# Chunked attention feeding a gated feed-forward layer: attn @ v joined with the next tile's scores, the last output tile in halves, and a new order of the plan

## The chip, the cores and the metric

The kernel runs on one core of a Trainium2 chip. The metric is the device time of one execution in microseconds (us), the median of three runs. TensorE (PE) does the matmuls, and PEld its weight loads; VectorE (DVE), ScalarE (ACT) and GpSimd (POOL) work element by element; SyncE (SP) only issues DMA transfers.

## The reference

```python
# q, k, v: (8, 8, 576, 64); chunks of 64 positions attend only to themselves
scores = scale * np.matmul(q_c, k_c.transpose(0, 1, 2, 4, 3))
scores = scores - np.max(scores, axis=-1, keepdims=True)
attn = np.exp(scores)
attn = attn / (np.sum(attn, axis=-1, keepdims=True) + 1e-09)
out = np.matmul(attn, v_c)
...
# x = out with the heads side by side: (8, 576, 512)
h = np.maximum(x @ w_in, 0.0)                 # (8, 576, 1024)
for k in range(K):                            # K = 3, a depthwise convolution along the sequence
    conv_out += conv_w[k][None, None, :] * hp[:, k:k + S, :]
gate = 1.0 / (1.0 + np.exp(-conv_out))
return (h * gate @ w_out).astype(np.float32)
```

## The kernel before

The 4608 rows of the sequence are cut in two ways. The attention and the output go in 36 **tiles** of 128 rows (two chunks of 64). The first product of the feed-forward layer, with its convolution and gate, goes in 16 **units** of 288 rows (half a batch), each in eight blocks f of 128 hidden channels.

A tile of attention is a chain of steps over all engines. Its q and k are loaded and transposed (`t_pe` on PE and `t_copy` on ACT for tiles 0 to 8, `t_dve` on DVE for the rest). Then come `scores` (16 matmuls of 64x64 on PE, line 171), `s_max` and `s_sub` on DVE, `s_exp` on ACT, `s_sum`, `s_eps` and `s_rec` on DVE, `s_norm` on POOL (line 203), `p_pe` (a transpose on PE, line 210), `p_copy` on ACT, `attn_v` (16 more matmuls of 64x64, line 223), and `x_hi` on ACT and `x_lo` on DVE (line 251), which write the result as a rounded part and a rest into `x_h` and `x_l`. The scores and the result of attn @ v live in the two halves of one PSUM tile, `sx`.

Block (u, f) is `mm1` (12 matmuls of 290 columns, line 260: three products of the split parts, four pieces of the contraction each). It then goes through ACT, DVE, ACT, DVE (`h_relu`, `c_mid`, `c_left`, `c_right`, `c_sig`, `c_mul`), and `g_hi` (ACT) and `g_lo` (POOL) split it into `g_h` and `g_l`. `mm1` of unit u waits for `x_lo` of every tile that the unit reads (tiles 0 to 2 for unit 0, 0 to 4 for unit 1). It holds one of six PSUM banks until `c_mul` is done. Output tile t takes eight steps `mm2` (three matmuls of 512 columns each, line 313), one for each f; when all are done, ACT copies the bank (`o_copy`, line 318) and SP stores it (`o_store`).

The weights come in over SP (`w_load`) and are split into high and low parts by six steps on DVE (lines 342 to 368), ACT and POOL. w_in comes in six pieces, in the order of the plan, and the last of them that SP issues is called wi3 here; w_out comes in four.

The order of all this is not left to the program text. Every step is entered with an engine, an estimated cost and a key. A planner then walks through the steps and gives each engine, at each time, the ready step with the lowest key; `by_step` and `by_chain` are tables of numbers that shift the keys by kind of step and by tile, block or output tile. `kinds` and `turn` charge PE for passing between 64x64 matmuls, transposes and large matmuls, and the key of a 64x64 step is lowered by 6 when the last step on PE was one too. Each engine then executes its instructions in the planned order, strictly. Where PE is idle in the plan and a bank is free, the program puts in transposes of the identity that nobody reads (line 685, called fillers here), until the first `mm2`:

```python
    pe_free, until_ = 2.0, min(begin[i] for i in range(n_) if steps[i]["fn"] is mm2)
    ...
            for _ in range(int((begin[i] - pe_free) / 0.14) if idle else 0):
                nc.tensor.transpose(out=banks[idle[-1]][:, 0:P], in_=ident, identity=ident)
```

Of the kernel before, what the change touches and what calls it, by code (L numbers as in the profile page):

```python
# [30 lines left out]
def attn_ffn(ctx: ExitStack, tc: tile.TileContext, q, k, v, w_in, conv_w, w_out, out):  # L31
    nc = tc.nc
    B, H, S, D = q.shape
    DM, DF = w_in.shape
# [194 lines left out]

    def x_views(st, t, x):  # L230
# [193 lines left out]
    def att(t, key, load_key, writes):  # L424
# [19 lines left out]
        s = step("PE", 0.47, key, scores, (st,), tt + [before.get("s")], take=[("sx", st, "s")], free=["qT", "kT"], bank="sx")  # L444
# [73 lines left out]

    for u in range(NU + 1):

        for t in tiles_for[u] if u < NU else []:
# [27 lines left out]
        "w_load": -4.5, "w_mask": -6, "w_bias": -5.5, "w_rest": -5, "w_low": -2, "w_sign": -9.5, "w_pow": -6,  # L549
        "<lambda>": -7, "c_sum": -23.5, "c_pe": 5, "c_copy": -31.5, "w_hi": 12, "w_lo_big": 20, "load_rows": -11,  # L550
        "t_pe": -7.5, "t_copy": -11, "load_v": 10.5, "scores": -3, "s_max": 8, "s_sub": -21.5, "s_exp": -9, "s_sum":
        -0.5, "s_eps": 2.5, "s_rec": 10, "s_norm": -19, "p_copy": -0.5, "attn_v": 4, "x_hi": -3, "x_lo": -6, "mm1":
        -0.5, "h_relu": -4.5, "c_mid": 2, "c_left": 2.5, "c_right": 2.5, "c_sig": 5, "c_mul": 6, "g_hi": 3, "g_lo":
        29.5, "o_copy": 6, "o_store": 16.5, "load_group": 35.5, "load_part": -3.5, "t_dve": 23
# [165 lines left out]
```

## Time and profile before

| | |
|---|---|
| median of 3 runs | 516.85 us (516.49 to 519.48) |
| profiled execution | 517.22 us, of which the span of the instructions is 515.4 us |
| busy share of the span | PE 98%, PEld 87%, DVE 68%, ACT 63%, POOL 33% |
| matmuls | 5104, at a mean granted clock of 0.999 |

The span runs from the first to the last instruction; the remaining 1.8 us of the execution lie around it. A share of busy time is a mean over stages that differ: in the first 90 us weights are split and DVE is nearly always busy, and afterwards PE is.

### The profile page before, as it was taken

What the parts mean: (1) busy time and instruction counts of PE and PEld (TensorE: products, weight loads), DVE (VectorE), ACT (ScalarE), POOL (GpSimd) and SP (SyncE); (2) the same over time, 40 slices, a digit from 0 to 9 for tenths busy, and PEclk for the clock granted to TensorE, in tenths of its full rate; (3) what the DMA queues carried; (4) which work ended last, traced back from release to release, by engine and by line L of the source; (5) the groups of instructions that cost most, each with busy time, mean ns of one, the idle gap of its engine ahead of it and who ended that gap; (6) DMA issues with size and microseconds to landing.
All of it is one profiled execution on the core that took longest, in us unless ns stands there. A gap on an engine that the chain in (4) does not pass through costs nothing.

```text
span 515.4 us, 13095 instructions
## 1 busy us (share of the span) xinstructions
PE 505.4 (98%) x5104; PEld 450.8 (87%) x5104; DVE 351.8 (68%) x732; ACT 325.1 (63%) x783; POOL 172.1 (33%) x237
## 2 busy tenths in 40 slices
PE   8898999999999999999999999999999999999997
PEld 8788988888998899899888898889889898988985
DVE  5779999668749588867854499727858585753320
ACT  4678998845866367757635487737746567755430
POOL 1424485532314323532511153314313315043220
PEclk9999999999999999999999999999999999999999
DMA  8889751543325545523455554343551211001101
GB/s 218 198 218 262 187 131 37 93 100 88 51 46 117 89 114 108 98 47 51 100 114 113 123 89 85 57 97 74 97 121 33 61 23 42 2 1 43 41 14 68
DMA packets 183170, 47.04 MB, mean 91 GB/s; under 512 B 175404, under 2 KB 175428, under 8 KB 183108
## 3 DMA queue, kind: packets, MB, share of 16 engines
q1 hardware_dynamic: 183108, 46.20, 40.5%
q8 instruction: 40, 0.66, 0.6%
q14 instruction: 22, 0.18, 0.1%
HBM read 36.72 MB, written 9.44 MB: 90 GB/s over the span
## 4 chain that ended last, share of the span: by engine, by line
PE 85%; DVE 8%; DMA 3%; ACT 2%; POOL 1%; issue 0%; SPq 0%; DVEq 0%; ACTq 0%; POOLq 0%
PE b_ps L313 38%; PE b_ps L260 37%; PE sx_ps L223 4%; PE sx_ps L171 3%; DMA qk<-in_moe_w_in 3%; PE b_ps L210 3%; DVE wt L360 1%; DVE wv L355 1%; POOL wv L376 1%; DVE wv L351 1%; DVE we L368 1%; DVE c L281 1%; DVE wt L342 1%; DVE c L290 1%; DVE x_l L251 1%; DVE c L275 1%
## 5 line engine op out<-in xcount | busy, mean ns | idle before, releaser
L304 POOL TENSOR_TENSOR g_l<-c,g_h 128x288 fp32r<-128x288 f32 (+8 forms) x184 | 114.7, 638 | 217.3 <-ACT g_h L300 209.8
L313 PE MATMUL b_ps<-wo_h,g_h 128*128 128x512 f32 x288 | 118.1, 410 | 0.0
L313 PE MATMUL b_ps<-wo_h,g_l 128*128 128x512 f32 x288 | 113.3, 393 | 0.0
L313 PE MATMUL b_ps<-wo_l,g_h 128*128 128x512 f32 x288 | 112.9, 392 | 0.0
L275 DVE SCALAR_TENSOR_TENSOR c<-b_ps,cw,c 128x288 f32<-128x288 f32 (+1 forms) x128 | 65.2, 512 | 62.7 <-ACT c L271 62.4
L260 PE MATMUL b_ps<-x_h,wi_h 128*128 128x290 f32 x512 | 91.5, 300 | 1.3 <-DVE c L290 1.3
L260 PE MATMUL b_ps<-x_l,wi_h 128*128 128x290 f32 x512 | 90.2, 298 | 0.0
L260 PE MATMUL b_ps<-x_h,wi_l 128*128 128x290 f32 x512 | 89.8, 297 | 0.0
L260 PEld LDWEIGHTS b_ps<-x_h,wi_h 128*128 128x128 f32 x512 | 77.3, 189 | 6.2 <-DVE c L290 2.3
L266 ACT ACTIVATE b_ps<-b_ps 128x290 f32<-128x290 f32 x128 | 50.7, 398 | 47.1 <-PE b_ps L260 46.4
L300 ACT CAST g_h<-c 128x288 fp32r<-128x288 f32 (+8 forms) x184 | 60.3, 358 | 26.9 <-DVE c L290 13.3
L260 PEld LDWEIGHTS b_ps<-x_h,wi_l 128*128 128x128 f32 x512 | 76.4, 190 | 0.0
L260 PEld LDWEIGHTS b_ps<-x_l,wi_h 128*128 128x128 f32 x512 | 76.3, 189 | 0.0
L290 DVE SCALAR_TENSOR_TENSOR c<-c,b_ps 128x288 f32<-128x288 f32 x128 | 57.2, 449 | 20.5 <-ACT c L287 18.8
L287 ACT ACTIVATE c<-c 128x288 f32<-128x288 f32 x128 | 56.5, 443 | 22.7 <-DVE c L281 21.5
L281 DVE SCALAR_TENSOR_TENSOR c<-b_ps,cw,c 128x287 f32<-128x287 f32 (+1 forms) x128 | 65.4, 514 | 2.9
L271 ACT ACTIVATE c<-b_ps,cw 128x288 f32<-128x288 f32 x128 | 63.3, 498 | 4.7 <-POOL g_l L304 0.4
L313 PEld LDWEIGHTS b_ps<-wo_h,g_l 128*128 128x128 f32 x288 | 54.1, 188 | 12.2
L203 POOL TENSOR_TENSOR e<-e,z 128x512 f32<-128x512 f32 x36 | 38.1, 1062 | 75.8 <-DVE z L200 62.5
L313 PEld LDWEIGHTS b_ps<-wo_h,g_h 128*128 128x128 f32 x288 | 54.2, 188 | 10.3
L313 PEld LDWEIGHTS b_ps<-wo_l,g_h 128*128 128x128 f32 x288 | 54.2, 188 | 8.6
L181 DVE TENSOR_REDUCE m<-sx_ps 128x8 f32<-128x512 f32 x36 | 24.6, 683 | 22.3 <-PE sx_ps L171 21.4
(48 smaller groups left out, 513.1 us busy)
## 6 DMA issues: line engine op xcount, KB each, us to landing
v<-in_v SPq DMA_DIRECT2D x144, 64.0 KB, 2.6
out<-wt SPq DMA_DIRECT2D x36, 256.0 KB, 2.4
qk<-in_q SPq DMA_DIRECT2D x96, 48.0 KB, 2.3
qk<-in_k SPq DMA_DIRECT2D x96, 48.0 KB, 2.3
qk<-in_moe_w_out SPq DMA_DIRECT2D x4, 1024.0 KB, 7.7
qk<-in_q SPq DMA_DIRECT2D x96, 24.0 KB, 1.9
qk<-in_k SPq DMA_DIRECT2D x96, 24.0 KB, 1.9
qk<-in_moe_w_in SPq DMA_DIRECT2D x4, 512.0 KB, 5.1
```

The lines of the kernel that those rows point to most:

```text
L181: nc.vector.tensor_reduce(out=st["m"], in_=st["sv"], op=ALU.max, axis=AX.X)
L203: nc.gpsimd.tensor_tensor(out=st["e"], in0=st["e"], in1=st["z"].rearrange("p (h o) -> p h o", o=1).broadcast_to([P, H, C]), op=ALU.mult)
L260: nc.tensor.matmul(h_ps[:, 0:XU], lhsT=wt[:, f // 2, kt, P * (f % 2):P * (f % 2) + P], rhs=xt[:, u % NX, kt, :], start=n == 0, stop=n == 3 ...
L266: nc.scalar.activation(out=banks[st["h"]][:, 0:XU], in_=banks[st["h"]][:, 0:XU], func=AF.Relu)
L271: nc.scalar.mul(out=st["c"], in_=banks[st["h"]][:, i0:i0 + HS], mul=cw[:, FT + f:FT + f + 1])
L275: nc.vector.scalar_tensor_tensor(out=c[:, a:HS], in0=banks[st["h"]][:, i0 + a - 1:i0 + HS - 1], scalar=cw[:, f:f + 1], in1=c[:, a:HS], op0 ...
L281: nc.vector.scalar_tensor_tensor(out=c[:, 0:b], in0=banks[st["h"]][:, i0 + 1:i0 + 1 + b], scalar=cw[:, 2 * FT + f:2 * FT + f + 1], in1=c[: ...
L287: nc.scalar.activation(out=st["c"], in_=st["c"], func=AF.Tanh, scale=0.5)
L290: nc.vector.scalar_tensor_tensor(out=st["c"], in0=st["c"], scalar=1.0, in1=banks[st["h"]][:, st["i0"]:st["i0"] + HS], op0=ALU.add, op1=ALU ...
L300: nc.scalar.copy(out=g_h[:, f, gs], in_=st["c"][:, cs])
L304: nc.gpsimd.tensor_tensor(out=g_l[:, f, gs], in0=st["c"][:, cs], in1=g_h[:, f, gs].bitcast(F32), op=ALU.subtract)
L313: nc.tensor.matmul(banks[st["o"]], lhsT=gt[:, f, o:o + P], rhs=wt[:, f, :], start=f == 0 and n == 0, stop=f == FT - 1 and n == 2)
```

## The change

From tile 8 on (`BOTH = 7`: the pair begins with attn @ v of tile 6 and the scores of tile 7), `scores` of a tile is no longer a step of its own. A step `both` issues the 16 matmuls of `attn_v` of the tile before and right behind them the 16 of `scores`; it is ready only when both are, and takes both halves of `sx`. Output tile 35 is computed in two halves of 256 columns, each in a bank of its own with its own copy and store. Fillers may go in until 110 us of the plan instead of until the first `mm2`. The planner takes two buffers of one pool for one step. All tables of keys are new, and steps whose key lies before 110 have a table of their own, which was a copy of the other before.

```diff
+    BOTH = 7
...
+    def both(st, before_):
+        attn_v(before_)
+        scores(st)
...
-    def mm2(st, t, f):
+    def mm2(st, t, f, m0=0, m1=DM):
         o = P * t % GR
         for n, (gt, wt) in enumerate(((g_h, wo_h), (g_h, wo_l), (g_l, wo_h))):
-            nc.tensor.matmul(banks[st["o"]], lhsT=gt[:, f, o:o + P], rhs=wt[:, f, :],
+            nc.tensor.matmul(banks[st["o"]][:, 0:m1 - m0], lhsT=gt[:, f, o:o + P], rhs=wt[:, f, m0:m1],
...
-        s = step("PE", 0.47, key, scores, (st,), tt + [before.get("s")], take=[("sx", st, "s")], free=["qT", "kT"], bank="sx")
+        after, take = tt + [before.get("s")], [("sx", st, "s")]
+        if t < BOTH:
+            s = step("PE", 0.47, key, scores, (st,), after, take=take, free=["qT", "kT"], bank="sx")
+        else:
+            b, tb, after_b, writes_b = before["x"]
+            s = step("PE", 0.94, key, both, (st, b), after + after_b, take=[("sx", b, "x")] + take,
+                     free=["qT", "kT", "pT", "v"], bank="sx")
+            x_steps(b, tb, s, key, writes_b)
...
+            cols = [(0, DM)] if t < NT - 1 else [(0, DM // 2), (DM // 2, DM)]
...
     by_step = {
-        "w_load": -4.5, "w_mask": -6, "w_bias": -5.5, "w_rest": -5, "w_low": -2, "w_sign": -9.5, "w_pow": -6,
+        "w_load": 23, "w_mask": -4, "w_bias": 24.5, "w_rest": 13, "w_low": -40.5, "w_sign": -28, "w_pow": -38,
...
     by_chain = [
-        9, -224, -167, -36, 12, -10, -96, 17, 35, 24, 31, 60, -46, -46, -16, 24, 26, 58, 8, -2, 35, 14, 36, 41, 0, -2,
+        -145, 322, -84, -153, -153, -69, -66, -56, -34, -30, -6, -21, -100, -74, -68, -10, -29, -22, -43, -62, -17, -54,
...
-    pe_free, until_ = 2.0, min(begin[i] for i in range(n_) if steps[i]["fn"] is mm2)
+    pe_free, until_ = 2.0, 110.0
```

What this does to the order, in three places. First, PE, around the scores of tile 9. Before, the scores of a tile (64x64 with kT and qT) can stand alone between large matmuls:

```order
L210 MATMUL b_ps<-ident,e 128x128 x4
L313 MATMUL b_ps<-wo_h,g_h 128x512
L313 MATMUL b_ps<-wo_l,g_h 128x512
L313 MATMUL b_ps<-wo_h,g_l 128x512
L171 MATMUL sx_ps<-kT,qT 64x64 x16
L313 MATMUL b_ps<-wo_h,g_h 128x512
```

After, they always follow attn @ v (64x64 with pT and v):

```order
L318 MATMUL b_ps<-wo_h,g_h 128x512
L318 MATMUL b_ps<-wo_l,g_h 128x512
L318 MATMUL b_ps<-wo_h,g_l 128x512
L224 MATMUL sx_ps<-pT,v 64x64 x16
L172 MATMUL sx_ps<-kT,qT 64x64 x16
L318 MATMUL b_ps<-wo_h,g_h 128x512
```

The 72 steps of this kind (36 of each) form 48 runs on PE before, of which 24 are pairs, and 42 after, of which 30 are.

Second, SP, the loads up to the last piece of w_in, wi3 (the last row of each). Before, it is issued behind the rows of tile 4 (loads of 64 partitions), another half piece of w_in and v of tile 2:

```order
L330 DMA qk<-in_moe_conv_w 24x256
L109 DMA qk<-in_q 64x8x64 x2
L109 DMA qk<-in_k 64x8x64 x2
L330 DMA qk<-in_moe_w_in 128x2x512
L141 DMA v<-in_v 64x4x64 x4
L330 DMA qk<-in_moe_w_in 128x4x512
```

After, the same loads stand ahead of it in another order; the other whole piece of w_in has come close to it, v of tile 2 and the rows of tile 4 lie between:

```order
L335 DMA qk<-in_moe_w_in 128x2x512
L110 DMA qk<-in_q 128x8x64
L110 DMA qk<-in_k 128x8x64
L335 DMA qk<-in_moe_w_in 128x4x512
L142 DMA v<-in_v 64x4x64 x4
L110 DMA qk<-in_q 64x8x64 x2
L110 DMA qk<-in_k 64x8x64 x2
L335 DMA qk<-in_moe_w_in 128x4x512
```

Third, ACT at the end of the program. Before, after the last blocks' steps, four output tiles are copied:

```order
L287 ACTIVATE c<-c 128x288
L300 CAST g_h<-c 128x160
L300 CAST g_h<-c 128x128
L318 ACTIVATE wt<-b_ps 128x512 x4
L716 UNCONDITIONAL_BRANCH
```

After, the two halves of tile 35 stand ahead of two whole tiles, 33 and 34, which end the program:

```order
L292 ACTIVATE c<-c 128x288
L305 CAST g_h<-c 128x160
L305 CAST g_h<-c 128x128
L323 ACTIVATE wt<-b_ps 128x256 x2
L323 ACTIVATE wt<-b_ps 128x512 x2
L740 UNCONDITIONAL_BRANCH
```

## Rows read from the trace of the kernel before

**Rows 1.** The page's chain of work that ended last: shares of the span by engine.
```profile
PE 85%; DVE 8%; DMA 3%; ACT 2%; POOL 1%; issue 0%; SPq 0%; DVEq 0%; ACTq 0%; POOLq 0%
```
**Rows 2.** Windows: busy us by engine (instructions), then clock, DMA share, GB/s.
```profile
0.00:37.07 37.07, 33.33 (x476) 30.56 (x477) 27.19 (x56) 22.81 (x40) 11.77 (x15) 1.00 0.88 212
37.07:59.57 22.50, 20.72 (x243) 19.75 (x242) 20.31 (x38) 19.05 (x42) 8.88 (x8) 1.00 0.84 216
59.57:90.00 30.43, 29.82 (x295) 26.06 (x294) 30.06 (x60) 26.68 (x57) 20.52 (x16) 1.00 0.46 112
90.00:511.44 421.44, 421.41 (x4099) 374.46 (x4097) 274.25 (x582) 255.96 (x647) 130.90 (x200) 1.00 0.35 72
```
**Rows 3.** What PE waited for, whole span: us in total, times, longest.
```profile
PE b_ps L260 <- DVE c L290: 1.3, 2, 0.8
PE b_ps L210 <- POOL e L203: 1.1, 2, 1.0
```
**Rows 4.** Timeline of PE: first blocks of unit 0, and the first of unit 1.
```profile
37.07 0.78 PE L260 MATMUL b_ps<-x_h,wi_h 128*128 128x290 f32 x4
37.69 0.71 PE L260 MATMUL b_ps<-x_l,wi_h 128*128 128x290 f32 x4
38.23 0.70 PE L260 MATMUL b_ps<-x_h,wi_l 128*128 128x290 f32 x4
...
59.57 0.65 PE L260 MATMUL b_ps<-x_h,wi_h 128*128 128x290 f32 x3
```
**Rows 5.** Timeline of DVE before the two starts of Rows 4.
```profile
36.33 0.84 DVE L251 TENSOR_TENSOR x_l<-sx_ps,x_h 128x136 fp32r<-128x136 f32 x3 [0.40 <-ACT x_h L247]
38.85 0.69 DVE L342 TENSOR_SCALAR wt<-qk 128x1024 uint32<-128x1024 uint32 x1 [1.69 <-DMA qk<-in_moe_w_in]
...
59.17 0.75 DVE L251 TENSOR_TENSOR x_l<-sx_ps,x_h 128x256 fp32r<-128x256 f32 x2
```
**Rows 6.** Timeline of PE: a lone `p_pe` and a lone `scores` between steps of `mm2`.
```profile
115.97 0.60 PE L210 MATMUL b_ps<-ident,e 128*128 128x128 f32 x4
116.32 0.48 PE L313 MATMUL b_ps<-wo_h,g_h 128*128 128x512 f32 x1
116.63 0.40 PE L313 MATMUL b_ps<-wo_l,g_h 128*128 128x512 f32 x1
116.87 0.39 PE L313 MATMUL b_ps<-wo_h,g_l 128*128 128x512 f32 x1
117.19 0.69 PE L171 MATMUL sx_ps<-kT,qT 64*64 64x64 f32 x32
117.82 0.50 PE L313 MATMUL b_ps<-wo_h,g_h 128*128 128x512 f32 x1
118.15 0.39 PE L313 MATMUL b_ps<-wo_l,g_h 128*128 128x512 f32 x1
```
**Rows 7.** Timeline of PE: two 64x64 steps side by side.
```profile
145.03 1.16 PE L223 MATMUL sx_ps<-pT,v 64*64 64x64 f32 x64
146.12 0.50 PE L313 MATMUL b_ps<-wo_h,g_h 128*128 128x512 f32 x1
146.46 0.39 PE L313 MATMUL b_ps<-wo_l,g_h 128*128 128x512 f32 x1
```
**Rows 8.** One window of Rows 2's view, where DMA was idle in part.
```profile
22.00:28.00 6.00, 5.72 (x102) 4.94 (x101) 5.72 (x14) 4.76 (x9) 3.25 (x3) 1.00 0.54 110
```
**Rows 9.** Timeline of PE and POOL: tile 12 from its scores to `p_pe`.
```profile
160.74 0.69 PE L171 MATMUL sx_ps<-kT,qT 64*64 64x64 f32 x32
161.36 0.50 PE L313 MATMUL b_ps<-wo_h,g_h 128*128 128x512 f32 x1
...
165.21 1.04 POOL L203 TENSOR_TENSOR e<-e,z 128x512 f32<-128x512 f32 x1
...
166.31 0.66 PE L210 MATMUL b_ps<-ident,e 128*128 128x128 f32 x4
```
**Rows 10.** Timeline of ACT: the last copy of an output tile.
```profile
511.70 0.60 ACT L318 ACTIVATE wt<-b_ps 128x512 f32<-128x512 f32 x1 [0.78 <-PE b_ps L313]
```

More of the change, by code (lines that the diff above doesn't have):

```diff
@@ L543, in attn_ffn @@
-            s = step("ACT", 0.58, key + 1, o_copy, (st,), [prev], take=["wt"], free=[("bk", "o")])
-            step("SP", 1.2, key + 2, o_store, (st, t), [s], free=["wt"], lag=0.8)
-    by_step_early = {
-        "w_load": -4.5, "w_mask": -6, "w_bias": -5.5, "w_rest": -5, "w_low": -2, "w_sign": -9.5, "w_pow": -6,
[L550 to L554, printed above, removed]
+            units = [v_ for v_ in range(NU) if HS * v_ < P * t + P and P * t < HS * v_ + HS]
@@ new lines, in attn_ffn @@
+            cols = [(0, DM)] if t < NT - 1 else [(0, DM // 2), (DM // 2, DM)]
+            for n, (m0, m1) in enumerate(cols):
+                st = {}
+                prev = None
+                for f in range(FT):
+                    key = U[u + 1] + (U[u + 2] - U[u + 1]) * (i + (n + f / FT) / len(cols)) / len(outs_in[u]) + 0.3
+                    prev = step("PE", 0.7 / len(cols), key, mm2, (st, t, f, m0, m1),
+                                [prev] + wo_done[f] + [g_done[v_, f] for v_ in units], take=[("bk", st, "o")] if f == 0 else [])
+                    mm2_of[t, f] = prev
+                s = step("ACT", 0.58 if n == 0 == len(cols) - 1 else 0.38, key + 1, o_copy, (st, m1 - m0), [prev], take=["wt"], free=[("bk", "o")])
+                step("SP", 1.2, key + 2, o_store, (st, t, m0, m1), [s], free=["wt"], lag=0.8 / len(cols))
@@ new lines, in attn_ffn @@
+    by_step_early = {
+        "w_load": -7.5, "w_bias": -3, "w_rest": 2, "w_low": 2.5, "w_sign": 1.5, "w_pow": -12, "<lambda>": 9.5, "c_sum":
+        10, "c_pe": 23, "c_copy": -4.5, "w_hi": 15.5, "w_lo_big": 1, "w_lo_copy": 12.5, "load_rows": -3.5, "t_pe": -7,
+        "t_copy": -6.5, "load_v": 1.5, "scores": 4.5, "s_max": 7, "s_sub": 8.5, "s_exp": -8, "s_sum": -6, "s_eps": -0.5,
+        "s_norm": 15.5, "p_pe": -1, "p_copy": -4, "attn_v": 11.5, "x_hi": 9, "x_lo": 4.5, "mm1": -5, "h_relu": 1.5,
+        "c_mid": 3.5, "c_left": 3.5, "c_right": 5, "c_sig": -1, "c_mul": 8, "g_hi": 0.5, "g_lo": -3.5, "mm2": 5,
+        "o_copy": -40, "o_store": -1.5, "both": 14, "load_group": 20, "load_part": -11, "t_dve": -25.5
@@ L562, in attn_ffn @@
-        29.5, "o_copy": 6, "o_store": 16.5, "load_group": 35.5, "load_part": -3.5, "t_dve": 23
+        "w_load": 23, "w_mask": -4, "w_bias": 24.5, "w_rest": 13, "w_low": -40.5, "w_sign": -28, "w_pow": -38,
+        "<lambda>": 11.5, "c_sum": -7.5, "c_pe": 7.5, "c_copy": 20, "w_hi": 19, "w_lo_big": -19, "w_lo_copy": -7.5,
+        "load_rows": 15, "t_pe": -0.5, "t_copy": 27, "load_v": -11.5, "scores": -11.5, "s_max": 9, "s_sub": 11, "s_exp":
+        1.5, "s_sum": 2.5, "s_eps": -5.5, "s_rec": -6.5, "s_norm": -32.5, "p_pe": -2, "p_copy": -3, "attn_v": -25,
@@ L563, in attn_ffn @@
+        "x_hi": -21.5, "x_lo": -1.5, "mm1": -1, "h_relu": -13.5, "c_mid": -1.5, "c_left": -3, "c_right": 2, "c_sig":
+        6.5, "c_mul": 2, "g_hi": -5, "g_lo": -26, "mm2": 1, "o_copy": -17, "o_store": 5, "both": -0.5, "load_group":
+        -14, "load_part": 31.5, "t_dve": 27.5
     }
     by_chain = [
[10 rows of a table removed]
[10 rows of a table added]
     ]
```

51 lines of the change are left out of this document (23 added, 28 removed), and 18 rows, old and new, of the table by_chain.

## The prediction

> **What bounds the kernel now.** I read the chain of waits first: 85% of the span lies on PE [rows 1]. The windows by stage then show which stage this holds for. From 90 us to the end of the matmuls PE is busy for 421.41 of 421.44 us, and the list of what PE waited for has only start-up entries [rows 2, 3]. From there nothing but PE's own work counts: how many matmuls there are, and what each change of shape costs. Before 90 us it is otherwise: from 59.57 to 90 DVE is busy for 30.06 of 30.43 us, and between 37.07 and 59.57 PE waits or runs fillers [rows 2, 3]. The two starts that matter there are set by DVE: the first block of unit 0 starts at 37.07, when `x_lo` of tile 2 (36.33, three instructions) ends, and unit 1 at 59.57, beside `x_lo` of tile 4 (59.17) [rows 4, 5]. DVE itself stood idle for 1.69 us before 38.85, until wi3, the last piece of w_in, had landed [rows 5]. So three things can move the time: the start of unit 1, PE's work from there on, and the tail.
>
> **PE's work: the 64x64 steps.** A lone `scores` begins 0.32 after the start of the matmul ahead of it, where 0.23 is the usual spacing (0.09 more), lasts 0.63 until the next start, and the next matmul takes 0.33 instead of 0.23: 0.09 + 0.63 + 0.10 = 0.82 [rows 6]. Two steps side by side take 1.09, and the next matmul 0.34; with the same 0.09 ahead that is 1.29 [rows 7]. A merge saves 2 x 0.82 - 1.29 = 0.35. The change makes 29 joined steps, but most tiles had a neighbour already: counted from the first block of unit 1, the order has 61 such steps in 39 runs before and in 32 after. Seven merges at 0.35 are **-2.45**. On the same stretch stand 33 transposes (`p_pe`, `t_pe`) before and 35 after; a lone one costs 0.35 + 0.08 = 0.43 [rows 6], so **+0.9**. Ten of them lean on a 64x64 step before and three after; each then shares a change of shape, about half of 0.09, so **+0.3**. Together **-1.2**. All of it is on the path, since PE never waits there. Changes between `mm1` and `mm2` have become more frequent, but both are 128x128 and I price them at 0: between the bounds of 0 and 0.1 for a few tens of them, since in [rows 6] only the other shapes lengthen a neighbour.
>
> **The halved tile.** 24 matmuls of 512 columns become 48 of 256. Four matmuls of 290 columns start 0.54 apart (38.23 - 37.69), 0.135 each [rows 4], and one of 512 takes 0.23 [rows 6]: 0.095 for 222 columns, 0.43 ns each, which leaves 0.01 us for the matmul itself. One of 256 is then 0.121, and 48 x 0.121 - 24 x 0.23 = **+0.3**. The ends: 0, if only columns count, and 48 x 0.135 - 5.5 = +1.0, if it is no faster than one of 290. I take 0.3, as both rows lie near. The Trainium skill (TensorEngine Tiling (Array Packing), section Instruction Overhead) gives about 60 cycles for each matmul; 24 more at 2.4 GHz would make an estimated 0.6 instead of 0.3, which these rows do not show. At the end the halves bring nothing: the order puts both of their copies ahead of the whole tiles 33 and 34. The last copy is again one of 512 columns, at 511.70 for 0.60 [rows 10], with a whole store behind it, so the tail keeps its length. The extra `o_copy` and `o_store` run on ACT and SP, which are idle in part there [rows 10]; if they were late, only banks would come free later, with no block left that needs one.
>
> **The start of unit 1.** It hangs on `x_lo` of tile 4, and that on DVE's queue from wi3's first step on. In both orders DVE has exactly the same instructions ahead of that step. Between it and `x_lo` of tile 4 there are 36 before, from 38.85 to 59.92, so 21.1 us or 0.58 each [rows 5], and 40 after: three long ones of w_out have gone, seven (two blocks' convolution and product, one `w_pow`) have come. This is between 0 and 4 x 0.58 = 2.3; six of the seven being short, I take **+0.7**. When wi3 lands is open. SP issues the same loads ahead of it in both orders. From 22 to 28 us DMA had a busy share of 0.54 [rows 8], so 6 x 0.46 = 2.8 us went unused; with the hole closed wi3 lands up to 2.8 earlier, with no change 0, and if the rows of tile 4, now directly ahead of it, hold SP up, about 1 later. I take half of the hole, **-1.4**. The start of unit 1 then moves by **-0.7**, between -2.8 and +1.7. PE reaches unit 0 sooner, by the fewer fillers in the order (158 ahead of it instead of 167, and one `scores` less), but waits the longer for unit 1: nothing of that comes through. Fillers themselves cost nothing as long as PE would wait. The later limit for them is empty: the order has none after unit 1 begins, before or after.
>
> **New waits.** `both` makes `scores` wait for `p_copy` of the tile before. Behind it on PE stand large matmuls that could have run; behind those, everything. The chain from the end of tile 12's scores (161.36) to its `p_pe` (166.31) takes 4.95, of which `s_norm` is the last 1.04 [rows 9], and PE had just enough other work between. In the new order, counted at the prices above, the shortest such distances are 4.4 (tiles 17 and 19), 4.8, 5.1, 5.1 and 5.3: waits of 0.55, 0.55 and 0.15 if the chain is as long. The bounds are 0 and 1.2; I take **+0.6**, since that chain had other work of DVE in it. Between 59.57 and 90 PE lost 30.43 - 29.82 = 0.6 [rows 2]; I leave it, with 0 and 2 as ends, since two pieces of w_out are now split later on DVE and the `mm2` that need them stand later too.
>
> **Sum.** -1.2 + 0.3 - 0.7 + 0.6 = -1.0 on the profiled execution of 517.22, so 516.2; that execution lay 0.37 above the median of 516.85, so 515.8 for the median. With all ends on one side it would be -4.6 or +4.7.
>
> **Rivals.** (1) *The start comes through whole.* wi3 lands 2.8 earlier, DVE follows without a hole, the 0.6 of waits before 90 us goes and no new wait comes: -1.2 + 0.3 - 2.8 - 0.6 = -4.3, or 512.5, and a little more if DVE's stretch is shorter than I think. For it speaks that the loads are in another order and that the hole is there; against it, that the loads of tile 4, with 64 partitions, lie in the hole and are still ahead of wi3. (2) *The chain of a joined step becomes the bound, slower.* `p_pe` waits for `s_norm`, behind it on PE stand the blocks, and the next `both` waits too. It decides from a chain longer than 4.95. With 6.0, the seven distances below that (4.4 to 5.8) cost 7.2 in all; with that in place of the 0.6 the sum is +5.6, or 522.4. For it speaks that DVE has other instructions between these steps; against it, that DVE is busy for only 274 of 421 us after 90 [rows 2], and that tile 12 had interruptions too. (3) *PE's clock falls in the start.* With 11 fewer fillers PE may stand idle for longer, and a lower clock would double the 8 blocks of unit 0: 8 x 1.62 = 13, less the 3 to 4 us of waits and fillers there, +9, or 526. The granted clock was 1.00 in each stage, also where PE waited for 1.0 at a time [rows 2, 3], which speaks against it. The Trainium skill (TensorE: Matmul & The Clock Gate, section Why this matters for your kernels) warns that an idle TensorE returns to half rate; by that rule only this rival would come about. (4) *The change does not do what it says*: the halves are not last, and the fillers' limit is without effect. Both are in the forecast already.
>
> **How the numbers follow.** The forecast has a chance of 0.72 and, with the bounds of its terms taken together in part, reaches from 513 to 519.5; rival 1 has 0.19, rival 2 0.07, rival 3 0.02. The range has to reach down to rival 1: 512.2 to 519.5. One per cent, 5.2 us, is about what a measurement of this kernel can tell from no change; below 511.7 lies about half of rival 1, 0.10, and above 522.0 most of rivals 2 and 3 and a little of the forecast's upper tail, 0.06. The rest is 0.84.
>
> **What would show it.** Right: unit 1 begins at 57 to 60 us, 32 runs of 64x64 steps after that, each pair at 1.29 with its neighbours; 48 matmuls about 0.12 apart for tile 35; a tail of 4 us after the last matmul, as before. PE's list of waits after 90 us holds about 0.6 us, under `s_norm`. Wrong: unit 1 before 56 us or after 62, long waits of `p_pe` for POOL, matmuls of 256 columns at over 0.14, or a granted clock below 1.00 before 90 us.

## The result, and the profile after

| | before | changed |
|---|---|---|
| median, us (20 executions each) | 517.0 (516.23 to 519.48) | 518.24 (516.21 to 520.42) |
| ratio to before, 95% interval | | 1.0022 [1.0012, 1.0033] |
| the same, measured again beside the experiments, twice | | 1.0034 [1.0018, 1.0050] and 1.0020 [1.0004, 1.0035] |
| profiled execution: time, span | 517.22, 515.4 | 519.21, 517.3 |
| first block of unit 0, of unit 1 | 37.07, 59.57 | 37.80, 61.63 |

The changed kernel is a little slower: 0.2 to 0.3%, inside the 1% that I called no difference and inside the range, but on the other side of the forecast. The page's chain of work that ended last has less PE and more DVE than in [rows 1]:

```profile
PE 83%; DVE 11%; DMA 2%; ACT 1%; issue 1%; POOL 1%; POOLq 0%; DVEq 0%; ACTq 0%
```

The windows by stage, cut at the same events as [rows 2], columns as there:

```profile
0.00:37.80 37.80, 32.91 (x436) 29.94 (x436) 26.27 (x54) 21.02 (x37) 10.10 (x15) 0.95 0.88 211
37.80:61.63 23.83, 20.61 (x265) 19.23 (x264) 22.68 (x44) 21.08 (x46) 13.18 (x9) 1.00 0.72 176
61.63:90.00 28.37, 27.71 (x289) 24.77 (x288) 28.23 (x53) 25.98 (x54) 18.73 (x15) 1.00 0.53 137
90.00:513.31 423.31, 422.94 (x4136) 377.76 (x4134) 277.19 (x585) 258.23 (x648) 132.88 (x201) 1.00 0.34 72
```

The second stage took 23.83 instead of 22.50, and DVE was busy in it for 22.68 instead of 20.31: DVE, not PE, set its end. In the first the granted clock was 0.95, where it had been 1.00. From unit 1 to the end of the last matmul it is 451.7 against 451.9 before: there the change is worth nearly what the forecast's other terms said together.

What PE waited for in the whole span (total, times, longest):

```profile
PE b_ps L211 <- POOL e L204: 3.5, 3, 2.6
PE b_ps L211 <- DVE c L295: 1.3, 1, 1.3
PE b_ps L265 <- DVE c L295: 1.1, 1, 1.1
```

Against [rows 3] a long wait for `s_norm` is new, 2.65 us. It stands in the start, ahead of `p_pe` of tile 0. The timeline of PE from there:

```profile
20.37 0.65 PE L211 MATMUL b_ps<-ident,e 128*128 128x128 f32 x4 [2.65 <-POOL e L204]
...
22.20 1.06 PE L150 MATMUL b_ps<-ident,qk 128*128 128x128 f32 x4
23.18 1.13 PE L224 MATMUL sx_ps<-pT,v 64*64 64x64 f32 x32
24.25 2.22 PE L709 MATMUL b_ps<-ident 128*128 128x128 f32 x12
26.40 0.69 PE L172 MATMUL sx_ps<-kT,qT 64*64 64x64 f32 x32
```

And two windows of the same stretch (the granted clock is the third number from the right):

```profile
22.00:24.00 2.00, 1.98 (x35) 1.61 (x37) 1.66 (x4) 1.25 (x3) 1.27 (x1) 0.57 0.97 253
24.00:26.00 2.00, 2.00 (x22) 1.88 (x19) 0.99 (x3) 1.61 (x3) 0.05 (x1) 0.57 1.18 237
```

After the wait the granted clock is 0.57, most of the time at the lower of its two levels (1.2 GHz): four transposes take 1.06 instead of 0.60, `attn_v` 1.13 instead of 0.69. This was rival 3's mechanism, and the first suspect.

The timeline of DVE ahead of wi3's first step and at `x_lo` of tile 4, for [rows 5]:

```profile
37.27 0.83 DVE L256 TENSOR_TENSOR x_l<-sx_ps,x_h 128x136 fp32r<-128x136 f32 x3
38.02 0.68 DVE L186 TENSOR_TENSOR e<-sx_ps,m 128x512 f32<-128x512 f32 x1
39.39 0.69 DVE L195 TENSOR_REDUCE z<-e 128x8 f32<-128x512 f32 x1 [0.70 <-ACT e L191]
40.00 0.68 DVE L347 TENSOR_SCALAR wt<-qk 128x1024 uint32<-128x1024 uint32 x1
...
61.25 0.74 DVE L256 TENSOR_TENSOR x_l<-sx_ps,x_h 128x256 fp32r<-128x256 f32 x2
```

The timeline of PE at the first block of unit 1, for [rows 4]:

```profile
61.63 0.79 PE L265 MATMUL b_ps<-x_h,wi_h 128*128 128x290 f32 x4
```

The wait of 1.69 for wi3 is gone. But `w_mask` of wi3 comes at 40.00, not earlier than 38.85; and from there to `x_lo` of tile 4 it is 21.25 instead of 20.32. (Both count to the start of `x_lo`'s first instruction; the table of all starts below counts to its end.) The load itself is hardly earlier: SP issued wi3 at 31.79 instead of 30.89, and it landed at 38.1 instead of 38.8, so in the changed kernel DVE came to it 1.9 us after it had landed. The idle time of DMA of [rows 8] was filled, but as much opened ahead of it. The window in front of [rows 8], in the kernel before:

```profile
16.00:22.00 6.00, 4.36 (x66) 4.30 (x67) 4.47 (x9) 3.89 (x7) 1.30 (x2) 1.00 1.08 235
```

And the two windows in the changed kernel (DMA's share is the number before the last):

```profile
16.00:22.00 6.00, 2.92 (x41) 2.38 (x30) 4.08 (x10) 1.66 (x3) 1.37 (x1) 1.00 0.54 121
22.00:28.00 6.00, 5.97 (x90) 5.26 (x91) 3.60 (x9) 3.60 (x7) 2.32 (x2) 0.72 1.05 285
```

The end is as long as before: the last copy starts 3.7 us before the span's end in both, and the halves' copies lie 9 us ahead of it. The timeline of ACT there, for [rows 10]:

```profile
504.23 0.74 ACT L323 ACTIVATE wt<-b_ps 128x256 f32<-128x256 f32 x2 [2.37 <-PE b_ps L318]
...
513.56 0.60 ACT L323 ACTIVATE wt<-b_ps 128x512 f32<-128x512 f32 x1 [0.78 <-PE b_ps L318]
```

So 2.06 us were lost by the start of unit 1, and 0.2 won behind it. Two theories for the loss. **Clock**: the wait for `s_norm` lowers PE's clock, so tile 2 comes late, and everything behind it too. **Queue**: whatever PE does, DVE's new order needs longer from the first piece of w_in that lands late (a half piece, called wi0a in the new order and wi0b in the old; the whole piece ahead of wi3 in the new order is called wi2) to `x_lo` of tile 4. The executions' own clocks seemed to speak for the first: of the changed kernel's 20, nine with a mean clock of 0.999 or 1.000 took 517.5 on average, the other eleven 518.9.

### The profile page after: what moved, and what is told of

Its sections match the earlier page's. It is cut to its first block, busy times and chain, and to the rows that moved or that the text cites. A ratio compares the mean times of both kernels' runs of the same rounds, so it can differ in the third digit from the quotient of the medians.

```text
span 517.3 us, 13124 instructions
## 1 busy us (share of the span) xinstructions
PE 504.3 (97%) x5117; PEld 451.7 (87%) x5117; DVE 354.4 (69%) x732; ACT 326.9 (63%) x784; POOL 174.9 (34%) x237
## 4 chain that ended last, share of the span: by engine, by line
PE 83%; DVE 11%; DMA 2%; ACT 1%; issue 1%; POOL 1%; POOLq 0%; DVEq 0%; ACTq 0%
PE b_ps L318 37%; PE b_ps L265 36%; PE sx_ps L224 4%; PE sx_ps L172 3%; PE b_ps L211 3%; DMA qk<-in_moe_w_in 2%; DVE wt L365 1%; DVE wv L360 1%; DVE wt L347 1%; DVE m L182 1%; DVE e L186 1%; DVE c L295 1%; DVE c L280 1%; DVE c L286 1%; DVE z L195 1%
## 5 line engine op out<-in xcount | busy, mean ns | idle before, releaser
L318 PE MATMUL b_ps<-wo_h,g_h 128*128 128x512 f32 (+1 forms) x296 | 118.7, 401 | 0.0
L318 PE MATMUL b_ps<-wo_l,g_h 128*128 128x512 f32 (+1 forms) x296 | 114.6, 387 | 0.0
L318 PE MATMUL b_ps<-wo_h,g_l 128*128 128x512 f32 (+1 forms) x296 | 114.5, 387 | 0.0
L318 PEld LDWEIGHTS b_ps<-wo_h,g_l 128*128 128x128 f32 x296 | 55.6, 188 | 11.9
L318 PEld LDWEIGHTS b_ps<-wo_h,g_h 128*128 128x128 f32 x296 | 55.7, 188 | 9.8
L318 PEld LDWEIGHTS b_ps<-wo_l,g_h 128*128 128x128 f32 x296 | 55.7, 188 | 7.9
(48 smaller groups left out, 515.4 us busy)
```

The costliest lines, as they stand in the source:

```text
L318: nc.tensor.matmul(banks[st["o"]][:, 0:m1 - m0], lhsT=gt[:, f, o:o + P], rhs=wt[:, f, m0:m1], start=f == 0 and n == 0, stop=f == FT - 1 an ...
```

## The experiments

All kernels of this section leave the computation as it is. An edit of the order sets the planned begin of a step, by which the program is then written out; `nth(f, n)` is step n of function f. The ratios are to the kernel before, in executions on the same chip.

**1. `fill`: fillers in the wait.**

```diff
     for i in sorted(order_, key=lambda i: begin[i]):
...
+        if i == nth(p_pe):
+            for _ in range(23):
+                nc.tensor.transpose(out=banks[steps[i]["args"][0]["pt"]][:, 0:P], in_=ident, identity=ident)
         steps[i]["fn"](*steps[i]["args"])
```

Expected: 

> The changed kernel with 23 more fillers ahead of p_pe of tile 0, where PE stood idle for 2.65 us; DVE's, ACT's, POOL's and SP's orders stay. Clock theory: the idle time ahead of 20.37 us makes the granted clock fall in part of the executions (11 of 20 of the changed kernel had a mean clock below 0.999, and a span 1.4 us longer, 517.0 against 515.6). With the gap filled every execution has 0.999 or 1.000, 22 to 26 us is at 1.00, scores of tile 2 begin at about 24.5 instead of 26.40, unit 1 begins at about 60.3 instead of 61.63, and the median falls by 0.7 to 1.2, to a ratio of 1.000 to 1.001 to the kernel before. Queue theory: PE's slow stretch is hidden behind DVE, whose order alone delays x_lo of tile 4; then unit 1 stays at 61.3 to 62 and the ratio at 1.002.

Measured: 518.31, ratio 1.0024 [1.0004, 1.0044]. The timeline of PE in this kernel, with the wait filled:

```profile
17.60 2.67 PE L716 MATMUL b_ps<-ident 128*128 128x128 f32 x23
20.43 0.66 PE L211 MATMUL b_ps<-ident,e 128*128 128x128 f32 x4 [0.16 <-POOL e L204]
...
24.97 0.69 PE L172 MATMUL sx_ps<-kT,qT 64*64 64x64 f32 x32
```

And its timeline of DVE at wi2's first step:

```profile
31.98 0.69 DVE L347 TENSOR_SCALAR wt<-qk 128x1024 uint32<-128x1024 uint32 x1 [1.27 <-DMA qk<-in_moe_w_in]
```

The clock stayed at 1.00 and tile 2's scores came 1.43 us earlier, but unit 1 only 0.29 (61.34): DVE now waited 1.27 for wi2's load instead. The clock as the main cause falls.

**2. `eps`: the two short steps ahead of the late load.**

```diff
+    begin[nth(s_eps)] = begin[nth(w_mask, 1)] - 2e-6
+    begin[nth(s_rec)] = begin[nth(w_mask, 1)] - 1e-6
```

Expected: 

> The changed kernel with s_eps and s_rec of tile 0 ahead of w_mask of wi0a on DVE, so that s_norm and p_pe of tile 0 do not wait for that load. If this one wait is the cause: no wait ahead of p_pe, the clock holds, and the median falls by 0.7 to 1.2 as with the fillers (ratio 1.000 to 1.001). If idle time of any cause lowers the clock: PE then waits as long a little later, for the rows of tile 2 and ahead of c_pe (22.02, whose data come from DVE at 21.69 to 21.97), about 3 us between 17.7 and 22.0 in all, the clock falls as before and the ratio stays at about 1.002.

Measured: 517.6, ratio 1.0023 [1.0008, 1.0038]. `p_pe` of tile 0 no longer waited, and PE waited 1.98 ahead of `c_pe` instead, as the second reading had it; yet the clock held in the profiled execution (five of the twelve executions lay below 0.999). Unit 1 began at 60.05, and here wi0a had landed at 16.37 instead of 17.85: the start moves with that landing. From it to the end of `x_lo` of tile 4 DVE took 44.04, 44.14 in the changed kernel.

**3. `xlo`: three `c_mul` behind `x_lo` of tile 4.** Their begins were set just behind that of `x_lo`.

Expected: 

> The changed kernel with the three c_mul that stand on DVE ahead of x_lo of tile 4 moved behind it, no other order changed. Queue theory: x_hi of tile 4 ends at 60.48, so x_lo can start there instead of at 61.25 and unit 1 begins 0.8 to 1.1 us earlier (60.5 to 60.8 instead of 61.63); the median falls by about 0.9, to a ratio of 1.0005. Clock theory alone, or if the banks that these c_mul free are what the blocks of unit 1 wait for next: no gain, ratio 1.002.

Measured: 518.89, ratio 1.0043 [1.0023, 1.0062]: no gain. The timeline of DVE in this kernel at `x_lo` of tile 4:

```profile
59.56 0.76 DVE L256 TENSOR_TENSOR x_l<-sx_ps,x_h 128x256 fp32r<-128x256 f32 x2 [0.28 <-ACT x_h L252]
```

And that of PE there, fillers and the first block of unit 1:

```profile
59.23 1.69 PE L715 MATMUL b_ps<-ident 128*128 128x128 f32 x14
60.68 0.78 PE L265 MATMUL b_ps<-x_h,wi_h 128*128 128x290 f32 x4
```

`x_lo` ended 42.87 after wi0a's landing instead of 44.14; 0.72 of the 1.27 lies behind wi3's first step, where the edit acts. But fillers kept PE until 60.68, and from there to the end of the span it was 456.5 instead of 455.7: an `mm2` at 71.06 now waited 0.38 for a `c_mul`; the other 0.4 I cannot place.

**4. `last`: the halves at the very end.** The last two of eight steps of both halves, their copies and stores behind all others.

Expected: 

> The changed kernel with the last two of eight steps of both halves of tile 35, their copies and stores put behind tiles 33 and 34, so that the halves are what ends last. If the tail goes with the size of copy and store: copy 0.37 instead of 0.60 and a store of 128 KB that lands 0.5 us sooner (1.7 against 2.2), so the tail after the last matmul shrinks from 4.0 to 3.3 us and the median by 0.7. If only the copy's length counts: 0.2. If nothing does: 0.

Measured: 519.71, ratio 1.0056 [1.0037, 1.0075]: none of the three readings. The timeline of ACT at this kernel's end:

```profile
512.71 0.60 ACT L323 ACTIVATE wt<-b_ps 128x512 f32<-128x512 f32 x1 [0.24 <-DMA out<-wt]
514.31 0.38 ACT L323 ACTIVATE wt<-b_ps 128x256 f32<-128x256 f32 x1 [1.00 <-DMA out<-wt]
```

Two copies waited for a store, since there are two tiles named `wt`. The timeline of PE in the same trace prices the halved matmul, where 30 stand in a row ahead of one of 512 columns:

```profile
496.65 0.28 PE L318 MATMUL b_ps<-wo_h,g_h 128*128 128x256 f32 x1
...
500.18 0.40 PE L318 MATMUL b_ps<-wo_h,g_h 128*128 128x512 f32 x1
500.41 0.40 PE L318 MATMUL b_ps<-wo_l,g_h 128*128 128x512 f32 x1
```

(500.18 - 496.65) / 30 = 0.118 each, against 0.23.

**5. `last2`: the same with tiles of their own.**

```diff
-        st["os"] = work.tile([P, 2 * DM], F32, name="wt")[:, 0:n]
+        st["os"] = work.tile([P, 2 * DM], F32, name="wt" if n == DM else "wv")[:, 0:n]
```

Expected: 

> The halves of tile 35 last, as before, but their copies take the tiles named wv, which nobody uses by then, instead of wt, of which there are two: in the first try both copies at the end waited for a store to free one (0.24 and 1.00 us). If these waits were the loss, the tail after the last matmul is 3.3 to 3.5 us instead of 4.0, and the ratio 1.0005 to 1.0015, below that of the changed kernel; if the stores themselves take turns at the end, it stays at 4.0 or above and the ratio at 1.002 to 1.004.

Measured: 517.99, ratio 1.0036 [1.0019, 1.0053]. From the start of the last matmul to the end it is 4.0 us (511.22 to 515.2) instead of 4.2 (513.08 to 517.3): the waits were the loss, and the halves' own gain is 0.2, too little for the ratio.

**6. `v0`: an earlier landing.**

```diff
+    begin[nth(load_v)] = begin[nth(w_load, 1)] + 1e-6
```

Expected: 

> The changed kernel with the four loads of v of tile 0 (256 KB) put on SP behind the load of wi0a instead of ahead of the rows of tile 1; no other order changed. Landing theory: from wi0a's landing to x_lo of tile 4 DVE needs 43.8 to 44.5 us in the four traces with that order, whatever PE does, so unit 1 moves with that landing (16.4 to 17.9 us). 256 KB less ahead of it at some 190 GB/s are 1.3 us: w_mask of wi0a at 15.1 to 16.6, unit 1 at 58.8 to 60.5, ratio to the kernel before 0.999 to 1.001. If the queue has no backlog when wi0a is issued at 10.96, it lands as before and nothing moves (1.002); if attn_v of tile 0 (21.7 to 23.2) comes to wait for v, unit 1 is later.

Measured: 518.3, ratio 1.0036 [1.0024, 1.0049]. wi0a landed at 16.54, 1.31 earlier than in the changed kernel's trace (if by this edit is not certain: 16.4 to 18.1 occur without it), but unit 1 began only 0.67 earlier. The timeline of DVE at wi2's first step shows the wait that took its place:

```profile
31.60 0.69 DVE L347 TENSOR_SCALAR wt<-qk 128x1024 uint32<-128x1024 uint32 x1 [1.60 <-DMA qk<-in_moe_w_in]
```

**7. `w3`: wi3 ahead of `s_sum` of tile 3.**

```diff
+    begin[nth(s_sum, 3)] = begin[nth(w_rest, 6)] + 1e-6
```

Expected: 

> The changed kernel with s_sum of tile 3 behind the first two steps of wi3 on DVE (w_mask, w_rest) instead of ahead of them; it waited 0.70 us there for s_exp of tile 3, which the two steps would cover. If wi3 has landed by then, as the closed hole before 40.00 suggests, w_mask of wi3 comes 1.3 us earlier after wi0a's landing (about 20.5 us instead of 21.6 to 22.1) and unit 1 0.7 earlier: ratio 1.001. If wi3 lands only shortly before 40.00, DVE waits for the load instead and nothing is gained: ratio 1.002.

Measured: 517.76, ratio 1.0032 [1.0016, 1.0048]. The timeline of DVE at wi3's first step in this kernel:

```profile
37.84 1.47 DVE L347 TENSOR_SCALAR wt<-qk 128x1024 uint32<-128x1024 uint32 x1 [0.23 <-DMA qk<-in_moe_w_in]
```

And that of POOL beside it:

```profile
36.35 2.41 POOL L381 TENSOR_TENSOR wv<-wv,we 128x1024 f32<-128x1024 f32 x1 [5.23 <-DVE we L373]
```

The step began 20.7 us after the landing, as expected if wi3 is there by then (it had just landed). But it took 1.47 instead of 0.69, POOL's `w_lo_big` running beside it until 38.76, and the gain was gone.

**8. `split`: every joined step taken apart.**

```diff
+        if steps[i]["fn"] is both:
+            attn_v(steps[i]["args"][1])
+            waiting.append(steps[i]["args"][0])
+            continue
         steps[i]["fn"](*steps[i]["args"])
+        if waiting and steps[i]["eng"] == "PE":
+            scores(waiting.pop())
```

Expected: 

> The changed kernel with each of the 29 joined steps taken apart again: attn_v at its place, scores of the next tile behind the PE step that follows. Price theory: a step alone costs 0.82 and a pair 1.29, so 29 x 0.35 = 10 us more, and since scores come one step (1.6 us or 0.7) later, p_pe waits for s_norm at the places with less than 6.5 us between them, up to another 8: ratio 1.020 to 1.035. If changes of shape cost less than read, only the waits: below 1.015.

Measured: 541.24, ratio 1.0469 [1.0451, 1.0488], more than either. In its trace a lone `attn_v` costs 0.82 and lone `scores` 0.83 with their neighbours (medians), a pair in the changed kernel 1.29: 29 x 0.36 = 10.4, as priced. PE's idle time behind 61.5 us grew from 1.0 to 8.7; most of it stands in this line of the list of PE's waits:

```profile
PE b_ps L211 <- POOL e L204: 6.5, 7, 1.7
```

PE's busy time from unit 1 to the end of the last matmul grew by 15.0 (465.7 instead of 450.7); some 4.6 us of that I cannot place.

**9 and 10. `oldstart`, `oldlast`: the old numbers for the start.** In the changed kernel `by_step_early`, and `by_chain` for the chains whose keys lie below 110, got the values of the kernel before; in `oldlast` the halves also stand last as in `last2`.

Expected: 

> The changed kernel (joined steps, halves, later limit of fillers, the numbers that order the late part), but with the numbers of the kernel before for everything that is ordered in the start, so that every engine has the order of before until past the start of unit 1 (PE's first 110 rows, DVE's first 137); behind that the order is planned anew, with 28 joined pairs beside large matmuls as in the changed kernel. If the new order of the start is what costs: DVE needs 42.5 us instead of 43.6 to 44.8 from the first late piece of w_in to x_lo of tile 4, unit 1 begins 1.0 to 1.6 us earlier than in the changed kernel at the same landing, and what is behind keeps its 451.5 to 451.9: ratio to the kernel before 0.998 to 1.000. If the joined steps or the halves are what costs, it stays at 1.002 or above.

Expected: 

> The same, with the last two steps of the halves of tile 35 behind all others and their copies in the tiles named wv. The two gains add if nothing is shared: the start 1.0 to 1.6, the tail 0.2 (3.98 us from the last matmul's start to the end of the span instead of 4.22, read with the halves last in the changed kernel): ratio 0.997 to 0.9995, the fastest of all. If the end of the program has a wait of its own, as in the first try with the halves last, it is no better than with the old start alone.

Measured: 519.8, ratio 1.0073 [1.0055, 1.0091], and 519.92, 1.0071 [1.0054, 1.0088]. The start did what the theory said: 41.20 and 41.26 us instead of 43.6 to 45.3, unit 1 at 58.05 and 59.44. But from there to the end it was 459.0 and 458.8 instead of 455.7: in the order behind the start, planned anew, PE waits for 3.1 us instead of 0.9 (1.4 of it for a bank ahead of one `p_pe`), and another 1.1 I cannot place.

**11 and 12. `after2`, `before2`: second looks.**

Expected: 

> The changed kernel once more, on the chip of the others, for the comparison and for a second look at its start. Both theories: ratio 1.001 to 1.003 again; from w_mask of wi0a to x_lo of tile 4 43.6 to 44.8 us as in the six traces with that order, whenever wi0a lands and whether PE's clock falls or not.

Expected: 

> The kernel before once more, for a second look at its start. If DVE's order sets the stretch from the first late piece of w_in to x_lo of tile 4, it is 42.5 us again, within 0.5, with the wait for wi3 still there; if the 42.56 was a lucky execution, it is 43.5 to 44.5 as with the new order.

Measured: the changed kernel 517.85, ratio 1.0034 [1.0018, 1.0050], 45.28 us from wi0a's landing at 17.92, above the 44.8 expected, with the clock at 0.50 from 22 to 28 us. The kernel before 516.0 in its one execution; its timeline of DVE at wi3 and at `x_lo` of tile 4:

```profile
37.64 0.69 DVE L342 TENSOR_SCALAR wt<-qk 128x1024 uint32<-128x1024 uint32 x1 [0.59 <-DMA qk<-in_moe_w_in]
...
57.97 0.75 DVE L251 TENSOR_TENSOR x_l<-sx_ps,x_h 128x256 fp32r<-128x256 f32 x2
```

41.11 us from the landing at 17.61, and the wait for wi3, on which my largest term stood, is 0.59 here, not 1.69.

**13 to 15. `hyb8`, `hyb9`, `hyb9l`: the old start with the new rest.** Here the planner gets the order itself, as a list of step numbers: that of before up to a seam, the changed kernel's behind it.

```diff
+    line = {e: iter([i for i in line if steps[i]["eng"] == e] + [None]) for e in early}
+    head = {e: next(l) for e, l in line.items()}
...
             picks = []
+            cand = [i for i in cand if i == head[e]]
```

Expected: 

> Every engine has the order of the kernel before up to the last block of unit 1 (its first 489 steps), and behind that the remaining steps in the changed kernel's order; tile 7's scores stay apart, so 27 pairs beside large matmuls remain of 28. If the start's order is the whole loss: unit 1 at 58.0 to 58.4 with the first late piece at 17.2 to 17.6, from there to the end of the span 455.3 to 456.0 (before 455.83, changed 455.7) plus up to 1 us at the seam: ratio 0.998 to 1.001. If an early unit 1 is always paid for later (DVE's queue, p_pe), PE's waits behind 60 us grow by 1.5 to 3: ratio 1.002 to 1.006.

Expected: 

> The same with the seam behind attn_v of tile 7 and p_pe of tile 8 (541 steps in the order of before; steps are joined from tile 9 on). The same two readings: 0.998 to 1.001 or 1.002 to 1.006; if only the seam costs, the two differ by its waits of 0.5 to 1 us.

Expected: 

> The second of these, with the last two steps of both halves of tile 35 behind all other matmuls and their copies in the tiles named wv: 0.2 us less than without (the tail from the last matmul's start 3.98 instead of 4.22), ratio 0.9975 to 1.0005, below the kernel before if the start's order is the whole loss.

Measured: 522.32, ratio 1.0120 [1.0107, 1.0133]; 521.24, 1.0093 [1.0067, 1.0120]; 520.42, 1.0074 [1.0060, 1.0089]. Unit 1 began at 59.38, 60.22 and 59.11, and each lost 4.6 to 5.0 us behind it, more than the seam was allowed. One long wait shows in each; the timeline of PE in `hyb8`:

```profile
119.47 0.66 PE L211 MATMUL b_ps<-ident,e 128*128 128x128 f32 x4 [2.58 <-POOL e L204]
```

And in `hyb9`:

```profile
124.10 0.78 PE L265 MATMUL b_ps<-x_h,wi_h 128*128 128x290 f32 x3 [2.59 <-ACT x_h L252]
```

The lists of waits hold another 0.7 to 1.1. Most of the remaining 2 us stands in the traces too. In `hyb8` it is fillers ahead of a joined step that waits for `p_copy`, in the timeline of PE:

```profile
109.22 2.24 PE L837 MATMUL b_ps<-ident 128*128 128x128 f32 x19
```

In `hyb9` and `hyb9l` PE's clock fell behind the long wait. The windows in `hyb9`:

```profile
124.00:126.00 2.00, 1.90 (x9) 1.84 (x10) 1.65 (x3) 0.65 (x2) 0.00 (x0) 0.63 0.31 49
126.00:128.00 2.00, 2.00 (x10) 2.00 (x10) 1.06 (x3) 0.83 (x4) 0.63 (x1) 0.52 0.32 51
```

Here PE sets the pace, and (0.37 + 0.48) x 2 = 1.7 us are lost. The one execution of each kernel with a mean clock of 1.000 took 518.76 and 518.46, the others 519.62 to 524.14. So the start's gain could not be carried to the end by either way of joining the orders; part of what hid it was the clock.

**16. `newstart`: the new numbers for the start in the kernel before**, without joined steps, halves and later limit.

Expected: 

> The kernel before (no joined steps, whole tile 35, its own limit of fillers), with the changed kernel's numbers for everything that is ordered in the start: each engine has the changed kernel's order until past the start of unit 1 (PE's first 117 rows, DVE's first 126). If the start's order is what makes unit 1 late: from w_mask of wi0a to the end of x_lo of tile 4 43.6 to 45.3 us, unit 1 at 60.3 to 62.9, as in the changed kernel, against 58.1 to 60.2 in the six traces with the old start. If the other edits do it: 41.1 to 43.4 us, 58 to 60.2. Its time says less, since the order behind the start is planned anew and has 45 runs of 64x64 steps instead of 39 (about 2 us): ratio 1.005 to 1.010.

Measured: 533.65, ratio 1.0336 [1.0303, 1.0369]; the order behind the start fits it far worse than expected. The start itself, in the timeline of DVE:

```profile
61.36 0.74 DVE L251 TENSOR_TENSOR x_l<-sx_ps,x_h 128x256 fp32r<-128x256 f32 x2
```

And in that of PE:

```profile
61.74 0.79 PE L260 MATMUL b_ps<-x_h,wi_h 128*128 128x290 f32 x4
```

43.99 us from the landing to the end of `x_lo`, unit 1 at 61.74: the late start comes with the numbers alone.

**17 and 18. `filllast`, `after3`: fillers and halves together, beside the changed kernel.**

Expected: 

> The changed kernel with 23 fillers in PE's wait for s_norm of tile 0, and with the halves' last steps at the very end and their copies in the tiles named wv. Against the changed kernel on the same chip: the clock falls in a sixth of the executions instead of in half of them, at 0.3 to 1.5 us each, so 0.2 to 0.6 less, and 0.2 less in the tail: 0.4 to 0.8 less together, ratio to the kernel before 1.001 to 1.002. If the clock's falls cost nothing by the end: 0.2 less.

Expected: 

> The changed kernel beside it on the same chip: ratio 1.002 to 1.003, and in about half of its executions a mean clock below 0.999.

Measured: 517.68, ratio 1.0020 [1.0009, 1.0032], and 517.42, ratio 1.0020 [1.0004, 1.0035]. The clock stayed at 0.999 or above in all compared executions of the first, and fell below in three of eleven of the second; by the end no difference is measurable. No kernel of this study is faster than the one before.

**All starts side by side**, from the timelines of the profiled executions (us). "Landing" is the start of `w_mask` of the first late piece of w_in (wi0b in the old order, wi0a in the new), for which DVE waits in nearly all; then to the start of `w_mask` of wi3, from there to the end of `x_lo` of tile 4, the first block of unit 1, and from that to the end of the span. `eps`, `xlo`, `v0` and `w3`, which move instructions or loads in it, are left out.

| start | landing | to wi3 | to `x_lo` 4 | unit 1 | to the end |
|---|---|---|---|---|---|
| old: before | 17.36 | 21.49 | 21.07 | 59.57 | 455.8 |
| before2 | 17.61 | 20.03 | 21.08 | 58.37 | 455.8 |
| oldstart | 17.20 | 20.11 | 21.09 | 58.05 | 459.0 |
| oldlast | 18.52 | 20.17 | 21.09 | 59.44 | 458.8 |
| hyb8 | 17.59 | 21.07 | 21.07 | 59.38 | 460.7 |
| hyb9 | 17.14 | 22.36 | 21.05 | 60.22 | 460.3 |
| hyb9l | 17.33 | 20.90 | 21.23 | 59.11 | 460.3 |
| mean of the old | 17.54 | 20.88 | 21.10 | 59.16 | |
| new: changed | 17.85 | 22.15 | 21.99 | 61.63 | 455.7 |
| after2 | 17.92 | 23.30 | 21.98 | 62.85 | 455.8 |
| after3 | 18.09 | 22.56 | 21.98 | 62.28 | 455.0 |
| newstart | 18.11 | 22.03 | 21.96 | 61.74 | 469.8 |
| fill | 17.91 | 21.81 | 21.98 | 61.34 | 455.7 |
| filllast | 18.04 | 21.62 | 21.97 | 61.28 | 454.9 |
| last | 16.77 | 21.73 | 22.81 | 60.96 | 456.5 |
| last2 | 17.11 | 21.59 | 21.98 | 60.32 | 454.9 |
| split | 16.50 | 23.36 | 21.99 | 61.49 | 478.3 |
| mean of the new | 17.59 | 22.24 | 22.07 | 61.54 | |

## Why the prediction was wrong

**The failed step is the start of unit 1**, predicted at -0.7 us; the two groups of traces put it at +2.4. Of its two terms the stretch from wi3 to `x_lo` of tile 4 was right: +0.7 forecast, 22.07 - 21.10 = +0.97 measured, and nearly the same in every trace (but for `last`, with a wait of 1.60 for w_out). The other, wi3's first step 1.4 us earlier, has the wrong sign: 22.24 - 20.88 = +1.36, with the first late piece landing alike (17.59 and 17.54).

That term was half of the 2.8 us of [rows 8], and it counted as a gain because DVE had waited 1.69 us for wi3 [rows 5]. Three things were wrong with it.

First, the idle time of DMA was not won, it moved: in the changed kernel DMA's share is 1.05 from 22 to 28 us, but 0.54 from 16 to 22, where it had been 1.08, and wi3 landed 0.7 us earlier instead of 1.4. In all the traces of the table it is no earlier: 38.6 us on average with the new start, 38.3 with the old. Second, the 1.69 was a wait of one execution: in the other six traces with the old start it is 0.28 to 1.18, or absent.

Third, with the wait for wi3 gone DVE does not come earlier, it waits elsewhere. "DVE has exactly the same instructions ahead of that step" was true, and so the time of that step is work plus idle time, wherever that lies: from the landing to wi3 DVE's idle time is 1.9 us on average with the old start and 3.0 with the new (for `x_hi` of tile 0, scores of tile 2, wi2's load at up to 2.15, and 0.70 for `s_exp` of tile 3 in each). That is 1.1 of the 1.36; the rest are instructions that take longer. The work is alike: the stretch holds 44 instructions with the old start and 38 with the new, a larger piece of w_in among them, but their median durations add up to 20.2 us in both. I had counted DVE's instructions in the order, but not what each of them waits for there. `fill`, `v0` and `w3` show how far this goes: each took one wait or the time ahead of one away, and wi2's load, or POOL beside the next step, took its place.

The **clock** of rival 3 did fall, which I had given 0.02, but for some 3.4 us (6.8 in `after2`) between 21 and 29 us and not in the blocks of unit 0, and its price is not 9 us: the four traces with the new start and a fallen clock need 44.5 us on average from landing to `x_lo` of tile 4, the five without 44.2. The eleven slower executions of the changed kernel were not slow by the clock alone: in the traces it falls where wi0a lands late (17.85 to 18.11, PE idle for 2.65 us or more) and holds where it lands at 16.4 to 17.5 or the wait is filled, so the two come together. It falls with the old start too: in `hyb9` and `hyb9l` the clock is 0.50 from 20 to 22 us. Leaving out all six traces with a fall in the start, the stretch to wi3 is 20.57 with the old start and 22.02 with the new, so the difference stays. The Trainium skill (TensorE: Matmul & The Clock Gate, section Why this matters for your kernels) says that an idle TensorE returns to half rate, and the trace agrees with it by the row of 0.57. What a fall costs hangs on who sets the pace: 0.3 us between the averages of 44.5 and 44.2 in the start, which DVE sets, and 1.7 us in `hyb9` at 124 us, where PE does.

**The other terms.** From unit 1 to the end of the last matmul the forecast's -1.2 + 0.3 + 0.6 = -0.3 met -0.2, and that is partly luck, as the terms are off in both directions. The price of a merge is confirmed by `split` (0.36; forecast 0.35). For the halved tile it is 48 x 0.118 - 24 x 0.23 = +0.14 (forecast +0.3). The Trainium skill (TensorEngine Tiling (Array Packing), section Instruction Overhead) gives some 60 cycles for each matmul, an estimated +0.6 here, which the row does not show. New waits of `p_pe`: one of 0.25 at 140 us, and one of 0.66 at 81 us that the traces of `after3`, `last2` and `filllast` lack; with a wait of 0.50 for a bank gone, PE's long waits behind the start of unit 1 grew by 0.4 (0.91 instead of 0.50), forecast 0.6. That leaves -0.7 for merges and transposes, forecast -1.2; where the 0.5 lies is open. Without the wait of 0.66 the stretch is 450.8 to 450.9 instead of 451.7. The tail: 0, as forecast. The later limit for the fillers is without effect, as said.

**The sum** of the traces, +2.4 - 0.2, is more than the 1.0 to 1.8 us that the three comparisons show. The profiled executions of the changed kernel all lay above their medians (by 1.0, 2.7 and 1.8 us), with a late landing and a fallen clock in each; the five traces of the new start in which the clock held begin unit 1 at 61.1, the five of the old at 59.0. The times show the same division: among executions with a mean clock of 0.999 or more the changed kernel lies 0.9 (`after2`) and 0.6 us (`after3`) above the kernel before on the same chip, among the others 1.9 and 2.0. Up to a microsecond between traces and times stays open. That the start's order is the cause of the late unit 1 is shown by both exchanges (`oldstart`, `newstart`). They exchange the order of all engines at once, so whether SP's loads or DVE's steps delay it is read from the traces and not tested. That the old start would make the changed kernel as fast as before, or faster, is not: with each of the orders tried behind it, its gain was lost again.

## What to carry to other kernels

A wait for a load in one profiled execution is a sample, not a price: take a second profile before building on it, and ask what the waiting engine would meet next if the load came sooner, since in a start where every queue is nearly full the next wait takes its place. When an order is moved, count for the engine that sets the stage the instructions and also what each waits for in its new place. And an order tuned as a whole may not be repaired by halves: in all six kernels here that join one start to another rest (`oldstart`, `oldlast`, the three `hyb`, `newstart`) the part behind the start took 3 to 14 us longer.

## What was not expected of the hardware

- The granted clock fell to half for some 3.4 us (6.8 in `after2`) after PE had idled for 2.65 to 2.9 us and then run only short steps; after idle times of 1.27 and 1.67 at the same place it stayed at 1.00. The idle time alone does not decide it in these traces: it fell after a wait of 2.59 in `hyb9` and `hyb9l` and held after one of 2.58 in `hyb8`, and behind the wait ahead of the scores at 17.7 us it fell after 1.76 us in `hyb9` and held after 1.73 in the kernel before.
- The same load, issued at the same time (10.95 to 11.01 us in `eps`, the changed kernel and `last`), landed between 16.4 and 17.8 us. A difference of the start stays to the end: `last2` begins unit 1 1.31 us earlier than the changed kernel, lacks its wait of 0.66 at 81 us, and is 1.95 us earlier at 100 us and 1.97 at 470.
- A DVE instruction of 128x1024 took 1.47 instead of 0.69 us while POOL worked on a tile of the same size.
